# Causal attention with a squared-activation FFN on one core: narrow score jobs in plain f32, fixed right-aligned probability tiles, first values on ScalarE

## The chip, the core and the metric

The kernel runs on one core of a Trainium2 chip. The metric is the device time of one execution in microseconds. Before the change three runs took 1117.45, 1113.68 and 1116.32 us: the median is 1116.32 us. The profile was taken on a further execution of 1113.66 us, whose span from the first to the last instruction is 1111.9 us.

## The reference

```python
scores = scale * np.matmul(q, k.transpose(0, 1, 3, 2))         # B, H, S, D = 8, 8, 576, 64; f32
cum = np.cumsum(np.maximum(s, 0.0), axis=-1)
bias = -(cum[:, :, :, None] - cum[:, :, None, :])
scores = np.where(causal, -1000000000.0, scores + np.minimum(bias, 0.0))
attn = softmax(scores)                                         # max subtracted, sum + 1e-9
x = (attn @ v), heads side by side                             # 4608 tokens x 512
h = x @ w_in                                                   # 512 x 2048
g = np.where(h >= 1, h, np.where(h <= -1, 0.0, (h + 1) ** 2 / 4))
y = g @ w_out                                                  # 2048 x 512
```

## The kernel before

**FFN.** Operands are split into two f16 parts, high and low, and each product is three matmuls (high·high, high·low, low·high). The tokens of a batch are cut in two halves of 320 and 256 (`HALF`). For each half `ffn_h` makes 16 blocks of 12 matmuls into PSUM (line 531), ScalarE and VectorE make the activation from it (lines 543, 546, 547), ScalarE and GpSimd split it (lines 557, 558), and `ffn_y` uses it in 12 matmuls (line 570).

**Attention.** A job is a pair of heads and one half of the queries: 64 jobs, for each batch four *narrow* ones (half 0: query tiles of 64, 128 and 128 rows that see 64, 192 and 320 keys) and then four *wide* ones (half 1: two tiles that see 448 and 576 keys). A job has slots k = 0 to 7: preparation (`att_prep`, k = 0), values (`v_prep`, k = 1), six score units (`scores`, k = 2 to 7, one tile of one head, 576 keys in two pieces of 288); at k = 3 the loads of the next job are issued (`att_load`), at k = 7 the output of the previous job is made (`att_out`, "px", line 476).

**How scores are made precise.** Jobs 0 to 7 (batch 0) use plain f32: one matmul with 66 contraction rows, 64 of them q and k and two rows that add the cumulative bias (rows of 8 and -8 against cum; line 408). On the chip such a matmul appears as two weight loads and two matmul instructions. All later jobs use the reduced format f32r in two matmuls: Q1 and K1 of 128 rows (line 413) and Q2 and K2 of 68 rows (line 414). For that, q and k are loaded twice, into both halves of the partitions (line 338), ScalarE rounds them (lines 353, 356, 357), VectorE forms the remainders (lines 358, 361; in jobs 8 to 11 line 361 is on GpSimd), and two small DMAs on ScalarE's queue bring the bias rows from `cumd`. Q1, K1, Q2, K2 and the raw tiles rq, rk have one buffer each.

**After the score.** VectorE adds the mask, takes the minimum and writes a probability tile "p" (line 419), ScalarE takes the exponential (line 430). "p" rotates in four buffers, and GpSimd writes 64 zero columns behind each one's keys (line 403). `weights_t` scales and splits into "pb" (lines 451 to 457), a DMA transposes pb into "pt", and px multiplies pt by the transposed values "vt". Scores and px share two PSUM buffers "s".

**Start.** While the attention of batch 0 runs, the f64 weights are loaded in 16 + 16 chunks of 512 KB ("wir", "wor"), decoded and split (class `Weights`). `s` is loaded, cut at zero and summed along the row ("cum"); job 0 takes its bias rows straight from the SBUF tile, the later f32 jobs from the copy `cumf` in DRAM.

**Order.** Each engine runs its instructions in a fixed order that is made when the program is built: a list scheduler follows the program's order and the stated priorities (`high_priority`, `issue_after`). SyncE issues nearly all DMAs, in order, and an instruction of its queue that waits holds back those behind it.

## Time and profile before

| | |
|---|---|
| Median of three runs | 1116.32 us (1113.68 to 1117.45) |
| Profiled execution: time, span | 1113.66 us, 1111.9 us |
| Share of the span busy: PE, DVE, ACT, POOL | 91%, 77%, 66%, 61% |
| Mean granted TensorE clock | 0.961 |
| DMA moved | 155.12 MB |

The page lists for each engine its busy time in us. PE is TensorE's matmuls, PEld its weight loads, DVE VectorE, ACT ScalarE, POOL GpSimd, SP SyncE. In a timeline, a row gives the start in us from the span's start, the length in us, the engine, the line and operation, output<-input with its shape and the number of instructions that were merged (x). A bracket at the end is idle time of that engine just before the row and what ended it. Ends of matmuls are modelled: a matmul's bar is longer than the step to the next one, so bars overlap, and the step is what one costs.

### The profile page before, as it was taken

Reading aid. Unit: us, or ns where it says so; the run is one execution under the profiler, and the core shown is the slowest. Engines: PE = TensorE matmul, PEld = TensorE weight load, DVE = VectorE, ACT = ScalarE, POOL = GpSimd, SP = SyncE. Lnnn points to the kernel's source line nnn. Section 1 sums busy time; section 2 is a strip of 40 time slices with the busy share of each in tenths; the row PEclk is TensorE's granted clock in tenths of the full one; section 3 lists DMA queues with packets and bytes.
Section 4 is the critical chain, followed back from the end, with each engine's and each line's share of the span. In section 5 each row is a group of like instructions: output and inputs, shape, how many; then the busy total and the mean of one; then the engine's idle time right before and its main releaser. Section 6 shows DMA issues by size and latency. Waiting matters only on the chain.

```text
span 1111.9 us, 25079 instructions
## 1 busy us (share of the span) xinstructions
PE 1010.4 (91%) x8496; PEld 775.8 (70%) x8496; DVE 855.7 (77%) x2327; ACT 728.3 (66%) x1703; POOL 673.6 (61%) x1171
## 2 busy tenths in 40 slices
PE   3467798799999999999999999899999999899998
PEld 1234456587768877777778877787777877787787
DVE  7977896788777877877778877787778887887533
ACT  4556786677567774767567775877577765777432
POOL 4664677776557655676557755666467665766422
PEclk9956899699999999999999999999999999999999
DMA  7776753777558763878468763987377763776400
GB/s 228 176 195 172 189 142 91 158 165 156 106 111 184 158 146 74 182 147 175 89 126 185 149 148 73 184 165 155 80 161 163 168 137 77 159 155 137 68 25 20
DMA packets 340928, 155.12 MB, mean 140 GB/s; under 512 B 290984, under 2 KB 322572, under 8 KB 340800
## 3 DMA queue, kind: packets, MB, share of 16 engines
q1 hardware_dynamic: 331200, 143.68, 60.3%
q10 hardware_dynamic: 9600, 9.84, 2.8%
q8 instruction: 67, 1.10, 0.4%
q14 instruction: 61, 0.50, 0.2%
HBM read 72.28 MB, written 9.88 MB: 74 GB/s over the span
## 4 chain that ended last, share of the span: by engine, by line
PE 59%; DVE 15%; DMA 7%; issue 7%; ACT 6%; POOL 5%; SPq 0%; ACTq 0%; DVEq 0%; POOLq 0%
PE y L570 25%; PE h L531 24%; PE px L476 4%; PE s L413 3%; PE s L414 3%; DVE pb L457 3%; DMA pt<-pb 3%; DVE p L419 2%; DMA wir<-in_moe_w_in_dram 2%; DMA wor<-in_moe_w_out_dram 2%; ACT u L543 2%; DVE Q L358 2%; DVE h L546 2%; ACT p L430 2%; POOL pb L451 1%
## 5 line engine op out<-in xcount | busy, mean ns | idle before, releaser
L531 PE MATMUL h<-x,WI 128*128 128x256 f16 (+1 forms) x3072 | 465.2, 290 | 14.3 <-DVE u L547 7.1
L570 PE MATMUL y<-g,WO 128*128 128x256 f16 (+1 forms) x3072 | 455.6, 287 | 6.1 <-POOL g L558 4.8
L531 PEld LDWEIGHTS <-WI 128*128 128x128 f16 x3072 | 291.5, 99 | 106.4 <-issue 23.3
L570 PEld LDWEIGHTS <-WO 128*128 128x128 f16 x3072 | 287.5, 98 | 92.4 <-issue 14.4
L558 POOL TENSOR_TENSOR g<-u,g 128x320 f16<-128x320 f32 (+1 forms) x256 | 205.9, 804 | 149.3 <-ACT g L557 148.6
L430 ACT ACTIVATE p<-p,mn 64x64 f32<-64x64 f32 (+4 forms) x320 | 179.4, 561 | 144.0 <-DVE mn L419 131.2
L543 ACT ACTIVATE u<-h,ub,us 128x320 f32<-128x320 f32 (+1 forms) x256 | 149.2, 583 | 122.1 <-PE h L531 116.1
L451 POOL TENSOR_SCALAR pb<-p,rs 64x128 f16<-64x128 f32 (+4 forms) x160 | 97.5, 609 | 193.8 <-DVE rs L447 122.5
L546 DVE SCALAR_TENSOR_TENSOR h<-h,ws,u 128x320 f32<-128x320 f32 (+1 forms) x256 | 132.4, 517 | 102.3 <-ACT u L543 99.7
L454 POOL TENSOR_TENSOR pb<-p,pb 64x128 f16<-64x128 f32 (+4 forms) x160 | 170.3, 1064 | 9.4
L457 DVE SCALAR_TENSOR_TENSOR pb<-p,rs,pb 64x128 f16<-64x128 f32 (+4 forms) x160 | 138.4, 865 | 42.4 <-POOL pb L451 42.2
L419 DVE CUSTOM_DVE_ANT_0 p<-s,mask 64x64 f32<-64x64 f32 (+4 forms) x320 | 134.5, 421 | 27.4 <-PE s L414 23.7
L413 PE MATMUL s<-K,Q 128*64 128x64 f32 (+1 forms) x336 | 127.0, 379 | 15.7 <-DVE mn L419 8.7
L547 DVE SCALAR_TENSOR_TENSOR u<-u,r,h 128x320 f32<-128x320 f32 (+1 forms) x256 | 130.3, 509 | 6.8 <-DVE h L546 0.5
L452 ACT ACTIVATE p<-p,rs 64x64 f32<-64x64 f32 (+4 forms) x160 | 89.5, 560 | 56.7 <-DVE rs L447 55.8
L557 ACT CAST g<-u 128x320 f16<-128x320 f32 (+1 forms) x256 | 108.0, 422 | 6.3 <-DVE u L547 6.3
L414 PE MATMUL s<-K,Q 68*64 68x64 f32 (+1 forms) x336 | 103.8, 310 | 3.0 <-DMA K<-cumd 2.9
L453 POOL TENSOR_SCALAR pb<-p 64x128 f16<-64x128 f32 (+4 forms) x160 | 92.6, 579 | 14.4 <-ACT p L452 11.4
L476 PEld LDWEIGHTS <-vt 128*64 128x64 f16 x1536 | 73.7, 114 | 32.7 <-issue 27.9
L476 PE MATMUL px<-pt,vt 128*64 128x256 f16 (+3 forms) x1536 | 84.7, 260 | 10.6 <-DMA pt<-pb 9.1
L413 PEld LDWEIGHTS s<-K,Q 128*64 128x64 f32 (+1 forms) x336 | 62.1, 185 | 26.5 <-DVE mn L419 7.2
L414 PEld LDWEIGHTS s<-K,Q 68*64 68x64 f32 (+1 forms) x336 | 62.7, 187 | 6.2 <-ACT p L452 1.8
(107 smaller groups left out, 984.5 us busy)
## 6 DMA issues: line engine op xcount, KB each, us to landing
rk<-in_k_dram SPq DMA_DIRECT2D x56, 288.0 KB
v<-in_v_dram SPq DMA_DIRECT2D x32, 288.0 KB
rq<-in_q_dram SPq DMA_DIRECT2D x56, 160.0 KB
rk<-in_k_dram SPq DMA_DIRECT2D x56, 160.0 KB
wir<-in_moe_w_in_dram SPq DMA_DIRECT2D x16, 512.0 KB
wor<-in_moe_w_out_dram SPq DMA_DIRECT2D x16, 512.0 KB
rq<-in_q_dram SPq DMA_DIRECT2D x56, 128.0 KB
...
```

The costliest lines, as they stand in the source:

```text
L413: T.matmul(sc[:R, :c1 - c0], Q1[:, hd, qo:qo + R], K1[:, hd, c0:c1], start=True, stop=False)
L414: T.matmul(sc[:R, :c1 - c0], Q2[:KC, hd, qo:qo + R], K2[:KC, hd, c0:c1], start=False, stop=True)
L419: ttr[0] = V.tensor_tensor_reduce(out=Pt[:R, c0:c1], in0=sc[:R, :c1 - c0], in1=mask[:R, mo:mo + c1 - c0], scale=-0.125 if j < F32_JOBS els ...
L430: A.activation(Pt[:R, :W], Pt[:R, :W], AF.Exp, bias=m2[:R], scale=-1.0, accum_out=sums[n, i][:R, hd:hd + 1])
L454: G.tensor_tensor(los[1], pw, his[1], ALU.subtract)
L457: V.scalar_tensor_tensor(los[0], pv, rs[:R, :1], his[0], ALU.mult, ALU.subtract)
L476: T.matmul(px[hd * D:(hd + 1) * D, lo:N], VT[:, vl * NB + j, hd * D:(hd + 1) * D], PT[:, 4 * j + 2 * hd + pl, lo:], start=(m == 0), stop=( ...
L531: T.matmul(h[:, :N], WI[4 * kt + ft // 4][:, wl, ft % 4 * P:(ft % 4 + 1) * P], x[:, kt, xl], start=(n == 0), stop=(n == 3 * NKT - 1),)
L543: first = A.activation(u, h[:, :N], AF.Relu, bias=ubi[b], scale=usc[b][:, fg:fg + 1]).ins
L546: V.scalar_tensor_tensor(h[:, :N], h[:, :N], wsc[b][:, fg:fg + 1], u, ALU.mult, ALU.max)
L558: G.tensor_tensor(g[:, 1], u, g[:, 0], ALU.subtract)
L570: T.matmul(ys[b, hf, m][:, :N], WO[8 * (m // 2) + ft // 2][:, wl, c0:c0 + P], g[:, gl], start=(ft == 0 and n == 0), stop=(ft == NFT - 1 an ...
```

## The change

- **Narrow jobs of all batches in plain f32** (`in_f32`): jobs 0 to 7 as before, and now also the four narrow jobs of batches 1 to 7, 28 jobs. Each of their score units is one f32 matmul of 66 rows in place of the two f32r matmuls; they have no preparation and no second copy of q and k. Their two bias rows of q and of k come ready from a wider `cumf` (four rows for each head: cum, 8, -8, cum), in one DMA for q and one for k. Wide jobs of batches 1 to 7 stay as they were.
- **Loads in two buffers**: q and k of a job lie in one tile "qk" with two buffers, which takes the place of rq, rk and of the two fixed f32 pairs.
- **Probability tiles**: three fixed tiles PS (128, 512 and 640 columns, two heads each) in place of the rotating "p". Keys are right-aligned, so that the 64 zero columns always lie at the tile's end and are written once, at the start. Tiles of 64, 192, 320, 448 and 576 keys use PS 128, 512, 640, 512, 640.
- **First values**: in pairs 0 to 3 (batch 0) the scaled values are made by two ScalarE activations in place of two GpSimd operations.
- **Smaller ones**: `cx` holds the four rows of cum; Q1 and Q2 have 256 columns in place of 320; the last two weight tiles WO share their place with K1; `K_POOL` is gone (line 361 is always on VectorE).

```diff
-K_POOL = range(12)
...
-    QF, KF = [], []
-    for i, (tq, tk) in enumerate((("rq", "rk"), ("q1", "k1"))):
-        QF.append(ap.tile([P, 2, NQ], F32, tag=tq, bufs=1, name=f"QF{i}"))
-        KF.append(ap.tile([P, 2, S], F32, tag=tk, bufs=1, name=f"KF{i}"))
+    NQ1 = HALF[1][1]
+
+    def qk_tile(name, N, W):
+        t = ap.tile([P, 2 * (N + W)], F32, tag="qk", bufs=2, name=name)
+        q, k = t[:, :2 * N], t[:, 2 * N:]
+        return t, q.rearrange("p (h n) -> p h n", h=2), k.rearrange("p (h n) -> p h n", h=2)
+
+    first = qk_tile("qk_first", NQ, NQ)
...
+    cx = ap.tile([P, 4, S], F32, tag="pt", bufs=2, name="cx")
+    G.memset(cx[:BH, 1], 8.0)
+    G.memset(cx[:BH, 2], -8.0)
...
-    cumf = dp.tile([BH, S], F32, name="cumf")
+    cumf = dp.tile([BH, 4, S], F32, name="cumf")
...
-        nc.sync.dma_start(cumf, cum[:BH])
+        A.copy(cx[:BH, 3], cum[:BH])
+        nc.sync.dma_start(cumf, cx[:BH])
...
+    P_LEN = (P, 4 * P, 5 * P, 4 * P, 5 * P)
+    PS = {}
+    for w in sorted(set(P_LEN)):
+        PS[w] = cp.tile([P, 2, w], F32, name=f"PS{w}")
+        G.memset(PS[w][:, :, w - D:], 0.0)
...
+    def in_f32(j):
+        return j < F32_JOBS or jobs[j][1] == 0
...
+        t, q, k = qk_tile(f"qk{n}_{hf}", N, W) if j else first
+        raws[n, hf] = q, k
+        for t_, src, c0 in ((q, qT, q0), (k, kT, 0)):
+            sv = src[b, h0:h0 + 2, :, c0:W].rearrange("h d n -> d h n")
+            for d0 in (0,) if in_f32(j) else (0, D):
+                LOADQ.dma_start(t_[d0:d0 + D], sv)
+        if not in_f32(j):
             return
...
+            LOADQ.dma_start(q[D:KF32], cumf[2 * n:2 * n + 2, :2, q0:W].rearrange("h r n -> r h n"))
+            LOADQ.dma_start(k[D:KF32], cumf[2 * n:2 * n + 2, 2:, :W].rearrange("h r n -> r h n"))
...
-        if jobs.index((n, hf)) < F32_JOBS:
+        if in_f32(jobs.index((n, hf))):
             return
...
-        (G if jobs.index((n, hf)) in K_POOL else V).tensor_tensor(
-            K2[:D, :, :W], rk[:D], K1[:D, :, :W].bitcast(F32), ALU.subtract
-        )
+        V.tensor_tensor(K2[:D, :, :W], rk[:D], K1[:D, :, :W].bitcast(F32), ALU.subtract)
...
-        G.tensor_scalar(VB[:, 0, :S], v, r, 1.0, ALU.mult, ALU.mult)
-        if n < V_POOL:
-            G.tensor_scalar(v, v, r, 1.0, ALU.mult, ALU.mult)
+        if n >= V_POOL:
+            G.tensor_scalar(VB[:, 0, :S], v, r, 1.0, ALU.mult, ALU.mult)
+        else:
+            A.activation(VB[:, 0, :S], v, AF.Copy, scale=r)
+            A.activation(v, v, AF.Copy, scale=r)
             G.tensor_tensor(VB[:, 1, :S], v, VB[:, 0, :S], ALU.subtract)
...
-        if c0 == 0:
-            Pt = ap.tile([P, SP], F32, tag="p", bufs=4, name=f"p{n}_{i}_{hd}")
-            pbs[n, i].append(Pt)
-            G.memset(Pt[:R, W:W + D], 0.0)
-        Pt = pbs[n, i][hd]
+        Pt = PS[P_LEN[i]][:, hd, P_LEN[i] - D - W:]
...
-        if j < F32_JOBS:
-            T.matmul(
-                sc[:R, :c1 - c0], QF[j % 2][:KF32, hd, qo:qo + R], KF[j % 2][:KF32, hd, c0:c1], start=True, stop=True
-            )
+        if in_f32(j):
+            q, k = raws[n, i // 3]
+            T.matmul(sc[:R, :c1 - c0], q[:KF32, hd, qo:qo + R], k[:KF32, hd, c0:c1], start=True, stop=True)
         else:
```

What this does to the order is shown at three places. The first is VectorE in batch 4, from the end of the first narrow job (mn_2_1 is its last score unit) to the first units of the second (mn_0_0, mn_0_1). "ISA" rows are the mask-and-minimum operation of line 419 (now 424) and the read of its result; L358 and L361 are the remainders. Before:

```order
L419 ISA p_2_1_7881,mn_2_1_0_7886<-s_2_1_0_7883,mask 128x320
L419 ISA mn_2_1_0_7886 128x1
L358 SCALAR_TENSOR_TENSOR Q_1822<-rq_0_7772,Q_1822 64x640
L361 TENSOR_TENSOR K_107<-rk_0_7773,K_1823 64x2x320
L446 TENSOR_SCALAR rs_2_7890<-sm_2_7851 128x2
L447 RECIPROCAL rs_2_7890<-rs_2_7890 128x2
L419 ISA p_0_0_7985,mn_0_0_0_7990<-s_0_0_0_7987,mask 64x64
L419 ISA mn_0_0_0_7990 64x1
L457 SCALAR_TENSOR_TENSOR pb_2_7889<-p_2_0_7852,rs_2_7890,pb_2_7889 128x3x128
L488 SCALAR_TENSOR_TENSOR x_1_7154<-px_1_7897,ex_5561,x_1_7154 128x256
L419 ISA p_0_1_8014,mn_0_1_0_8019<-s_0_1_0_8016,mask 64x64
```

The same stretch after the change:

```order
L424 ISA mn_2_1_0_7602 128x1
L551 SCALAR_TENSOR_TENSOR h_1_0_7647<-h_1_0_7647,ws_6234,u_1_0_7661 128x256
L552 SCALAR_TENSOR_TENSOR u_1_0_7661<-u_1_0_7661,r_6224,h_1_0_7647 128x256
L451 TENSOR_SCALAR rs_2_7606<-sm_2_7573 128x2
L452 RECIPROCAL rs_2_7606<-rs_2_7606 128x2
L493 SCALAR_TENSOR_TENSOR x_0_7632<-px_0_7613,ex_7095,x_0_7632 128x320
L424 ISA PS_146,mn_0_0_0_7685<-s_0_0_0_7683,mask 64x64
L424 ISA mn_0_0_0_7685 64x1
L462 SCALAR_TENSOR_TENSOR pb_2_7605<-PS_150,rs_2_7606,pb_2_7605 128x3x128
L551 SCALAR_TENSOR_TENSOR h_1_1_7690<-h_1_1_7690,ws_6234,u_1_1_7703 128x256
L552 SCALAR_TENSOR_TENSOR u_1_1_7703<-u_1_1_7703,r_6224,h_1_1_7690 128x256
L424 ISA PS_146,mn_0_1_0_7711<-s_0_1_0_7709,mask 64x64
```

The remainders L358 and L361 are gone from between the two jobs; FFN work (L551, L552) and the other operations stand there in another order.

The second place is TensorE where batch 1 begins. Before, the last score units of batch 1's first narrow job stand one behind the other, directly ahead of the px of batch 0's last wide job (s is a score tile, px that output, pt its transposed weights):

```order
L413 MATMUL s_1_0_0_1907<-K_1823,Q_1822 128x192
L414 MATMUL s_1_0_0_1907<-K_107,Q_106 128x192
L413 MATMUL s_1_1_0_1932<-K_1823,Q_1822 128x192
L414 MATMUL s_1_1_0_1932<-K_107,Q_106 128x192
L413 MATMUL s_2_0_0_1961<-K_1823,Q_1822 128x320
L414 MATMUL s_2_0_0_1961<-K_107,Q_106 128x320
L413 MATMUL s_2_1_0_1971<-K_1823,Q_1822 128x320
L414 MATMUL s_2_1_0_1971<-K_107,Q_106 128x320
L476 LDWEIGHTS vt_666
```

After the change the units of that job, one matmul each, stand singly among the matmuls y of batch 0's FFN; here is one of them (s_1_0_0), and the px comes later:

```order
L575 LDWEIGHTS WO_136
L575 MATMUL y_0_3_1681<-g_0_8_1126,WO_136 128x320
L415 MATMUL s_1_0_0_1819<-qk_0_1603 128x192
L575 LDWEIGHTS WO_137
L575 MATMUL y_0_2_1680<-g_0_8_1126,WO_137 128x320
```

Between the last score of batch 0 (s_4_1_288 of its last job) and the px that uses it there were 20 FFN matmuls before, and there are 94 now.

The third place is the start of SyncE's queue (wir is a weight chunk, QF, KF or qk_first the tiles of job 0, cum or cx the row sums). Before:

```order
L120 DMA st<-in_s_dram 64x576
L322 DMA QF_77<-in_q_dram 64x2x320
L322 DMA KF_78<-in_k_dram 64x2x320
L190 DMA wir_155<-in_moe_w_in_dram 128x1024
L190 DMA wir_157<-in_moe_w_in_dram 128x1024
L190 DMA wir_159<-in_moe_w_in_dram 128x1024
L326 DMA QF_77<-cum 1x16x20
L327 DMA KF_78<-cum 1x16x20
L326 DMA QF_77<-cum 1x16x20
L327 DMA KF_78<-cum 1x16x20
L255 DMA v_0_161<-in_v_dram 128x576
```

After:

```order
L123 DMA st<-in_s_dram 64x576
L341 DMA qk_0_227<-in_q_dram 64x2x320
L341 DMA qk_0_227<-in_k_dram 64x2x320
L341 DMA qk_first<-in_q_dram 64x2x320
L341 DMA qk_first<-in_k_dram 64x2x320
L198 DMA wir_158<-in_moe_w_in_dram 128x1024
L347 DMA qk_first<-cx 1x16x20
L348 DMA qk_first<-cx 1x16x20
L347 DMA qk_first<-cx 1x16x20
L348 DMA qk_first<-cx 1x16x20
L198 DMA wir_160<-in_moe_w_in_dram 128x1024
L198 DMA wir_162<-in_moe_w_in_dram 128x1024
```

The load of s has moved to the front, and the second and third weight chunk stand behind the four bias rows, which wait for the row sums.

More of the change, by code (lines that the diff above doesn't have):

```diff
@@ L123, in attention_ffn @@
     V.memset(zr, 0.0)
-    V.memset(QF[0][D:KF32], 8.0)
-    V.memset(KF[0][D:KF32], -8.0)
+    V.memset(first[1][D:KF32], 8.0)
+    V.memset(first[2][D:KF32], -8.0)
+    cx = ap.tile([P, 4, S], F32, tag="pt", bufs=2, name="cx")
+    G.memset(cx[:BH, 1], 8.0)
+    G.memset(cx[:BH, 2], -8.0)
     V.tensor_scalar(st[:BH], st[:BH], 0.0, None, ALU.max)
-    cum = ap.tile([P, S], F32, tag="raw", name="cum")
+    cum = cx[:, 0]
     V.tensor_tensor_scan(cum[:BH], st[:BH], zr, 0.0, ALU.add, ALU.add)
-    cumf = dp.tile([BH, S], F32, name="cumf")
+    cumf = dp.tile([BH, 4, S], F32, name="cumf")
     cumd = dp.tile([BH, 2, S], F32, name="cumd")
@@ L148, in attention_ffn @@
     G.memset(ones, 1.0)
-    Q2 = cp.tile([P, 2, NQ], F32R, name="Q2")
+    Q1 = cp.tile([P, 2, NQ1], F32R, name="Q1")
+    Q2 = cp.tile([P, 2, NQ1], F32R, name="Q2")
     K2 = cp.tile([P, 2, S], F32R, name="K2")
@@ L163, in attention_ffn @@
     WI = [cp.tile([P, 2, NC], F16, name=f"WI{c}") for c in range(NW)]
-    WO = [cp.tile([P, 2, NC], F16, name=f"WO{c}") for c in range(NW + WO_LAG)]
+    WO = [cp.tile([P, 2, NC], F16, name=f"WO{c}") for c in range(NW)]
+    lag = ap.tile([P, WO_LAG, 2, NC], F16, tag="k1", bufs=1, name="WO_lag")
+    WO += [lag[:, i] for i in range(WO_LAG)]
     def flat32(t):
@@ L310, in attention_ffn @@
     NP = B * NPAIR
-    raws, pts_, vts, pbs, sums = {}, {}, {}, {}, {}
+    raws, pts_, vts, sums = {}, {}, {}, {}
+    def in_f32(j):
+        return j < F32_JOBS or jobs[j][1] == 0
     def att_load(n, hf):
@@ L318, in att_load @@
         j = jobs.index((n, hf))
[L319 to L339 removed]
+        t, q, k = qk_tile(f"qk{n}_{hf}", N, W) if j else first
[5 more added lines that the diff above has]
+        if not in_f32(j):
+            return
+        if j < CH_N:
+            for hd in range(2):
+                r = cum[2 * n + hd:2 * n + hd + 1]
+                LOADQ.dma_start(q[D:D + 1, hd], r[:, q0:W])
+                LOADQ.dma_start(k[D + 1:D + 2, hd], r[:, :W])
+        else:
+            LOADQ.dma_start(q[D:KF32], cumf[2 * n:2 * n + 2, :2, q0:W].rearrange("h r n -> r h n"))
+            LOADQ.dma_start(k[D:KF32], cumf[2 * n:2 * n + 2, 2:, :W].rearrange("h r n -> r h n"))
     def att_prep(n, hf):
[L343 removed]
+        if in_f32(jobs.index((n, hf))):
             return
         if not one:
[L346 removed]
             one.append(ap.tile([P, 2, S], F32R, tag="k1", bufs=1, name="K1"))
[L348 removed]
+        K1, = one
         rq, rk = raws.pop((n, hf))
@@ L420, in scores @@
                 out=Pt[:R, c0:c1], in0=sc[:R, :c1 - c0], in1=mask[:R, mo:mo + c1 - c0],
-                scale=-0.125 if j < F32_JOBS else -1.0, scalar=3.0e38 if mn is None else mn[:R],
+                scale=-0.125 if in_f32(j) else -1.0, scalar=3.0e38 if mn is None else mn[:R],
                 op0=ALU.add, op1=ALU.min, accum_out=m2[:R],
@@ L447, in weights_t @@
         V.reciprocal(rs[:R], rs[:R])
-        tiles2 = pbs.pop((n, i))
-        pv, pw = (Pt[:R, :W + D].rearrange("p (j c) -> p j c", c=P) for Pt in tiles2)
+        heads = [PS[P_LEN[i]][:R, hd, P_LEN[i] - D - W:] for hd in range(2)]
+        pv, pw = (t.rearrange("p (j c) -> p j c", c=P) for t in heads)
         his, los = ([PB[:R, :, 2 * hd + l, :] for hd in range(2)] for l in range(2))
         G.tensor_scalar(his[0], pv, rs[:R, :1], 1.0, ALU.mult, ALU.mult)
-        A.activation(tiles2[1][:R, :W], tiles2[1][:R, :W], AF.Copy, scale=rs[:R, 1:])
+        A.activation(heads[1][:, :W], heads[1][:, :W], AF.Copy, scale=rs[:R, 1:])
         G.tensor_scalar(his[1], pw, 1.0, 1.0, ALU.mult, ALU.mult)
```

28 lines of the change are left out of this document (2 added, 26 removed).

## The prediction

> **What bounds the kernel now.** I read the page's busy shares first, then the windows of three stretches (start, steady, last FFN): columns are the stretch, its length, and the busy us of PE, PEld, DVE, ACT and POOL.
>
> ```profile
> PE 1010.4 (91%) x8496; PEld 775.8 (70%) x8496; DVE 855.7 (77%) x2327; ACT 728.3 (66%) x1703; POOL 673.6 (61%) x1171
> 0.00:304.00 304.00, 231.23 (x1578) 156.81 (x1579) 244.58 (x622) 200.66 (x427) 193.78 (x310) 0.87 0.67 163
> 304.00:1041.00 737.00, 712.68 (x6339) 563.80 (x6337) 586.69 (x1658) 504.34 (x1224) 461.17 (x837) 1.00 0.67 141
> 1041.00:1112.00 71.00, 66.49 (x584) 55.23 (x582) 24.40 (x49) 23.30 (x53) 18.69 (x25) 0.99 0.10 27
> ```
>
> The steady stretch is six batches. PE is busy 712.7 of 737 us there at full granted clock (1.00), VectorE 80%, ScalarE 68%, GpSimd 63%: TensorE bounds it, and a microsecond of matmul that is added is paid in full unless it fills a wait. The first 304 us are different: VectorE leads (80%), PE is busy 76% at a clock of 0.87, and chains of latency count. In the last stretch there is no attention left, so the change does nothing there.
>
> So the question is which waits PE still has. The list of waits of PE in the steady stretch (us in total, times, longest):
>
> ```profile
> PE s L413 <- DVE Q L358: 6.3, 6, 1.7
> PE s L413 <- DVE mn L419: 6.0, 8, 1.2
> PE y L570 <- POOL g L558: 4.8, 6, 1.3
> PE s L414 <- DMA K<-cumd: 2.9, 2, 1.8
> PE px L476 <- DMA pt<-pb: 1.6, 2, 1.3
> PE px L476 <- DVE Q L358: 1.1, 1, 1.1
> ```
>
> They fill almost all of the 24.3 us in which PE is idle. Three of them (6.3, 2.9, 1.1) are the f32r preparation, and the 6.0 behind the minimum is its follower: VectorE runs in order, and in the first place shown above the remainders L358 and L361 stand ahead of the minimum that frees a score buffer. These two take
>
> ```profile
> L358 DVE SCALAR_TENSOR_TENSOR Q<-rq,Q 64x640 fp32r<-64x640 f32 x28 | 25.9, 925 | 2.5 <-ACT Q L353 1.6
> L361 DVE TENSOR_TENSOR K<-rk,K 64x640 fp32r<-64x640 f32 x24 | 19.9, 827 | 0.6
> ```
>
> **The price: f32 passes.** What a unit costs PE is the step from where the matmuls ahead of it end to the start of the next group. FFN steps first, then an f32r unit of 320 keys and one of 64, then an f32 unit of 448:
>
> ```profile
> 543.96 1.63 PE y L570 x12
> 605.94 1.47 PE L570 MATMUL y<-g,WO 128*128 128x256 f16 x12
> 607.25 0.27 PE L531 MATMUL h<-x,WI 128*128 128x256 f16 x1
> 569.79 0.84 PE L570 MATMUL y<-g,WO 128*128 128x320 f16 x5
> 570.36 0.42 PE L413 MATMUL s<-K,Q 128*128 128x320 f32 x1
> 570.62 0.30 PE L414 MATMUL s<-K,Q 68*128 68x320 f32 x1
> 570.77 1.12 PE L570 MATMUL y<-g,WO 128*128 128x320 f16 x7
> 564.36 0.71 PE L531 MATMUL h<-x,WI 128*128 128x320 f16 x4
> 564.79 0.30 PE L413 MATMUL s<-K,Q 128*64 128x64 f32 x1
> 564.93 0.22 PE L414 MATMUL s<-K,Q 68*64 68x64 f32 x1
> 564.99 1.27 PE L531 MATMUL h<-x,WI 128*128 128x320 f16 x8
> 110.74 0.92 PE L408 MATMUL s<-KF,QF 66*128 66x448 f32 x2
> 111.49 1.79 PE L531 MATMUL h<-x,WI 128*128 128x320 f16 x12
> L413 PEld LDWEIGHTS s<-K,Q 128*128 128x128 f32 x280 | 54.4, 194 | 14.6 <-PE s L414 4.5 <-DVE mn L419 3.7 <-DVE x L488 0.3
> ```
>
> An FFN matmul of 320 columns steps 1.63/12 = 0.136 us, one of 256 (607.25 - 605.94)/12 = 0.109. The five before the 320-key unit end at 569.79 + 5 x 0.136 = 570.47, so the f32r unit costs 570.77 - 570.47 = 0.30. The four before the 64-key unit end at 564.90: 0.09. By interpolation 192 keys cost 0.19. A narrow job (two heads) costs 2 x (0.09 + 0.19 + 0.30) = 1.16 us when nothing waits.
>
> The f32 unit of 448 keys steps 111.49 - 110.74 = 0.75 us, that is 1.67 ns a key: 0.11, 0.32 and 0.54 for the three narrow units, 1.93 us a job. This is the lower bound. The upper one lets each of a unit's two passes wait for a weight load of 0.194: 0.39, 0.39, 0.54, or 2.63 a job. At 448 keys no load shows at all, and the narrow units' weights are no bigger, so I stay near the lower end: 2.05. The increase is 0.89 us a job (0.77 to 1.47), for 28 jobs 24.9 us (21.6 to 41).
>
> Those short passes are where a rule weighs in. The Trainium skill, "TensorE: Matmul & The Clock Gate", section "The mechanism" (Part 3), says that a weight load overlaps running matmuls only if it goes to another row group. All passes here use the same rows; with every load of 0.194 in series a narrow f32 job would take 1.93 + 12 x 0.194 = 4.3 us, 2.2 more than the 2.05 I take, and the time would be 1101 + 28 x 2.2 = 1163. The row disagrees: two passes and two loads fit in 0.75 us, just the 448-column streaming. I give it 1 in 100.
>
> **The return: waits of the narrow jobs.** Lower bound, from the list: 6.3 + 6.0 + 2.9 + 1.1 = 16.3 us over 24 jobs, 0.68 a job. The list understates, since a matmul's bar is 0.30 long for a step of 0.136: each wait shows some 0.16 short. Upper bound, from a whole period:
>
> ```profile
> 912.42 1.63 PE y L570 x12
> 574.21 1.51 PE L476 MATMUL px<-pt,vt 128*64 128x256 f16 x30
> 575.65 0.24 PE L413 MATMUL s<-K,Q 128*64 128x64 f32 x1
> 611.69 0.94 PE L476 MATMUL px<-pt,vt 128*64 128x320 f16 x18
> 612.56 0.61 PE L531 MATMUL h<-x,WI 128*128 128x256 f16 x4
> ```
>
> The same piece of the chain comes at 543.96 and three batches later at 912.42: 122.8 us a batch. PE needs 384 x 0.136 + 384 x 0.109 = 94.1 for the FFN, 4 x (1.44 + 0.87) = 9.2 for px, 4 x 1.16 = 4.6 for the narrow scores, and scaled by columns (0.42 for 448, 0.27 for 288) 4 x 1.92 = 7.7 for the wide ones: 115.6. So 7.2 us a batch are lost, 1.8 a narrow job if all of it were theirs. Between 0.68 and 1.8 I take 1.2: the preparation waits and the hidden part of each, while waits for g and pt stay. Steady stretch: 24 x (0.89 - 1.2) = **-7.4 us**.
>
> **The start.** Batch 1 begins with PE idle:
>
> ```profile
> 194.57 0.63 PE L413 MATMUL s<-K,Q 128*128 128x320 f32 x1 [2.31 <-DVE mn L419]
> 202.15 2.77 PE L476 MATMUL px<-pt,vt 128*64 128x256 f16 x30 [5.62 <-DMA pt<-pb]
> 7.78 0.61 SPq L326 DMA_DIRECT2D QF<-cum  x1
> cumf<-cum SPq DMA_DIRECT2D x1, 144.0 KB
> ```
>
> In the second place shown, 94 FFN matmuls (12.8 us at 0.136) now lie between the last scores of batch 0 and their px, in place of 20 (2.7 us). They cover both waits: -7.9. The other three narrow jobs of batch 1 return less than a steady job each, -3 together; the four cost 4 x 0.89 = +3.6. In the first microseconds the third place counts: chunks two and three, issued before the bias row of 7.78, now go after four of them, a few us later; `cumf` grows from 144 to 576 KB, 432 KB more at the 163 GB/s of the start, 2.7 us of transfer. Against it the row sums start earlier, since s is loaded first. Bounds -1 and +6; I take +2. Sum of the start: -7.9 - 3 + 3.6 + 2 = **-5.3 us**.
>
> **Edits I cost at nothing.** Rows of the groups by shape:
>
> ```profile
> L403 POOL MEMSET p<- 128x64 f32 x256 | 34.6, 151 | 10.9 <-DVE pb L457 9.7
> L374 POOL TENSOR_SCALAR v<-v,rc 128x576 f32<-128x576 f32 x4 | 4.0, 992 | 0.2
> L452 ACT ACTIVATE p<-p,rs 128x576 f32<-128x576 f32 x32 | 24.8, 776 | 8.7 <-DVE rs L447 8.7
> ```
>
> The zero columns were 320 memsets of about 151 ns, 48 us of a GpSimd that is idle 39% of the span; FFN work hides them, and without that cover they would have been worth at most those few of them that PE feels. PS gives the narrow tiles three places in place of two and the wide ones two as before, so no new wait for a buffer. The values on ScalarE are 8 activations of about 0.78 us (nearest shape, L452), 6.2 us beside a ScalarE that is idle a third of the start; GpSimd loses operations of up to 0.99. Behind them on ScalarE wait exponentials and weight decodes: -1 to +2. Half the bytes of 28 loads go, at a DMA share of 0.67, and two buffers let them come a job earlier: 0, or up to the 1.6 us of waits for pt.
>
> **Sum.** 1113.66 - 7.4 - 5.3 = 1101.0. The profiled execution is 2.7 us below the median of 1116.32, about the spread of the runs, so I say 1102.
>
> **Rivals.**
> *The passes stay, the waits too (slower).* The waits behind the minimum may come from the two score buffers shared with px, not from the remainders; then only 6.3 + 2.9 + 1.1 = 10.3 us return, 0.43 a job. Steady: 24 x (0.89 - 0.43) = +11; with the start at 0, 1125; with loads in part exposed, 1139. It decides from a return under 0.89 a job. For it: 8 of the listed waits, 6.0 us, name the minimum and not the preparation. Against it: the order has VectorE free of the remainders just there. 20%.
> *The start takes it back.* Chunks come late to the engine that leads there (+6), y runs dry later in place of px (only -4 returned), the steady part is even: 1113.66 + 6 - 4 - 3 + 3.6 - 2 = 1114. 14%.
> *All lost time returns.* 24 x (0.77 - 1.8) = -25, start -9: 1080. Speaks for it: the units now stand singly between FFN groups. 10%.
> *Weight loads in series*, as above: 1163. 1%.
>
> **How the numbers follow.** My forecast (1088 to 1111) has 55%. Within 0.3% means 1113.0 to 1119.7, about what a measurement of this kernel can tell from no change. Faster is the forecast and the full return: 0.65. Same is the start's rival: 0.14. Slower is the first rival and the series of loads: 0.21. The range 1082 to 1127 leaves out about the lower half of the full return and the worse half of the slower cases.
>
> **What would show it.** Right: no wait of PE for Q or K in the list; 320-key f32 units stepping 0.54 us; a period under 122.8 us; PE idle at 190 to 215 us gone. Wrong: units of 64 and 192 keys stepping 0.39 (loads exposed); waits behind the minimum still 6 us or more; a first FFN matmul later than before; a period above 122.8.

## The result and the profile after

The changed kernel takes **1121.75 us** (median; 1119.29 to 1124.24, and 1129.54 in the profiled execution) against 1116.32 before. One more execution, of 1220.48 us at a mean granted clock of 0.857, belongs to a slower state and is left out of the range. The ratio is 1.0055, with a 95% interval of 1.0040 to 1.0070: slower, by about 6 us. The forecast was 1102. Measured again unmodified, beside the kernel before, it took 1126.88 against 1117.56, ratio 1.0079 (1.0054 to 1.0105).

The profiled execution lies 7.8 us above the median, so the second run's profile (1121.41) is read beside it. First the page of the changed kernel, busy time of each engine:

```profile
PE 1042.0 (92%) x8494; PEld 781.6 (69%) x8496; DVE 809.9 (72%) x2275; ACT 688.0 (61%) x1628; POOL 622.5 (55%) x842
```

VectorE, ScalarE and GpSimd each do 40 to 51 us less work than before; TensorE does 32 us more. Now the windows of the three stretches. So that the same work stands in each, the steady stretch is cut by the FFN itself: from 46.4 us after the first h matmul of batch 1 to 41.8 us after that of batch 7, which are the marks 304 and 1041 of before. The first three rows are the changed kernel, then the steady stretch of its second run:

```profile
0.00:298.60 298.60, 236.79 (x1580) 158.95 (x1582) 229.68 (x621) 198.90 (x424) 176.40 (x220) 0.89 0.71 163
298.60:1056.30 757.70, 739.22 (x6340) 568.07 (x6339) 556.74 (x1608) 466.02 (x1152) 429.84 (x600) 0.99 0.62 127
1056.30:1127.20 70.90, 66.05 (x578) 54.59 (x575) 23.45 (x47) 23.07 (x52) 16.24 (x23) 1.00 0.05 18
294.90:1048.10 753.20, 735.65 (x6340) 566.20 (x6339) 556.74 (x1608) 466.27 (x1152) 429.96 (x600) 1.00 0.62 128
```

The start is 5.4 us shorter (304.0 to 298.6; 9.1 in the second run). The steady stretch is 16.2 us longer in the second run: TensorE is busy 735.65 us in place of 712.68, **23.0 more**, and idle 17.5 in place of 24.3, only **6.8 less**. The forecast had 21.4 more and 28.8 less there: a return larger than all the idle time that the list showed.

What is left of the idle time is told by the list of waits of PE in the steady stretch of the changed kernel:

```profile
PE y L575 <- POOL g L563: 9.7, 6, 2.9
PE y L575 <- ACT g L562: 4.3, 7, 1.8
PE s L415 <- DVE mn L424: 2.3, 7, 0.5
PE px L481 <- DMA pt<-pb: 0.6, 1, 0.6
PE s L418 <- DVE mn L424: 0.5, 1, 0.5
```

Every wait for Q or K is gone, and the wait behind the minimum fell from 6.0 to 2.8. Scores and px waited 18.1 us before, now 3.4. But **y now waits 14.0 us for g** (13.7 in the second run), where it waited 6.0 before, 4.8 of them for GpSimd and the rest for ScalarE:

```profile
PE y L570 <- ACT g L557: 1.2, 6, 0.2
```

A new wait has come in place of the old ones, at other matmuls. It has two parts: for GpSimd's g 9.7 us (7.6 in the second run), for ScalarE's 4.3 (6.1).

**GpSimd's part.** Most of the 9.7 sits at one place, in five of the six batches: where the last narrow job gives way to the first wide one. The timeline of the changed kernel there (start, duration, engine; in brackets the wait ahead of it and for whom):

```profile
606.92 2.55 SPq L463 DMA_TRANSPOSE pt<-pb  x2
...
609.59 1.49 PE L536 MATMUL h<-x,WI 128*128 128x256 f16 x12
...
611.38 0.58 POOL L456 TENSOR_SCALAR pb<-PS,rs 128x384 f16<-128x384 f32 x1 [3.08 <-DMA pt<-pb]
...
612.53 1.09 POOL L459 TENSOR_TENSOR pb<-PS,pb 128x384 f16<-128x384 f32 x1
613.59 1.29 POOL L563 TENSOR_TENSOR g<-u,g 128x256 f16<-128x256 f32 x2
...
614.30 1.07 PE L575 MATMUL y<-g,WO 128*128 128x256 f16 x6 [2.15 <-POOL g L563]
615.66 2.57 PE L536 MATMUL h<-x,WI 128*128 128x256 f16 x11
```

There are two buffers pb for a narrow job's three query tiles, so the third tile (128x384) waits until the transpose of the first has read its buffer. In the trace GpSimd takes its work in order: behind that wait stand two splits of g, and y waits for the first. GpSimd waited for pt before as well, but y hardly behind it; the sums of the steady stretch are, before and in the second run:

```profile
POOL pb L451 <- DMA pt<-pb: 6.5, 6, 2.4
POOL pb L456 <- DMA pt<-pb: 8.2, 3, 3.1
```

In the first profile of the changed kernel it is 16.4. In the second run y waits for GpSimd at five turns, and GpSimd for pt ahead of three of them only.

**ScalarE's part.** It sits some 13 us earlier, where ScalarE rounds k for the first wide job. In the second run, last batch of the steady stretch:

```profile
961.24 0.70 PE L415 MATMUL s<-qk 66*128 66x320 f32 x2
961.97 0.62 SPq L341 DMA_DIRECT2D qk<-in_q_dram  x1
...
966.11 1.25 SPq L341 DMA_DIRECT2D qk<-in_k_dram  x2
...
971.17 1.15 ACT L367 CAST K<-qk 128x1152 fp32r<-128x1152 f32 x1 [1.95 <-DMA qk<-in_k_dram]
...
972.69 0.39 ACT L562 CAST g<-u 128x256 f16<-128x256 f32 x1
...
973.13 1.75 PE L575 MATMUL y<-g,WO 128*128 128x256 f16 x12 [1.64 <-ACT g L562]
```

An f32 score reads the load tile qk itself. So the load of the first wide job can go only after the last score of the narrow job that had its buffer (the bar ends at 961.94, the load goes at 961.97). By the trace it is such a score that releases this load in five of the six batches. ScalarE then waits for k, with the activation of the FFN behind it, and y waits for that. ScalarE's waits for k are 8.9 us in the steady stretch of the second run and were 0.2 before:

```profile
ACT K L367 <- DMA qk<-in_k_dram: 8.9, 6, 3.0
ACT K L356 <- DMA rk<-in_k_dram: 0.2, 1, 0.2
```

### The profile page after: what moved, and what is told of

It reads as the page before. It is cut to its first block, busy times and chain, and to the rows that moved or that the text cites. A ratio compares the mean times of both kernels' runs of the same rounds, so it can differ in the third digit from the quotient of the medians.

```text
span 1127.2 us, 24261 instructions
## 1 busy us (share of the span) xinstructions
PE 1042.0 (92%) x8494; PEld 781.6 (69%) x8496; DVE 809.9 (72%) x2275; ACT 688.0 (61%) x1628; POOL 622.5 (55%) x842
## 5 line engine op out<-in xcount | busy, mean ns | idle before, releaser
L435 ACT ACTIVATE PS<-PS,mn 64x64 f32<-64x64 f32 (+4 forms) x320 | 178.8, 559 | 143.6 <-DVE mn L424 115.4
L456 POOL TENSOR_SCALAR pb<-PS,rs 64x128 f16<-64x128 f32 (+4 forms) x160 | 106.7, 667 | 194.5 <-DVE rs L452 147.8
L551 DVE SCALAR_TENSOR_TENSOR h<-h,ws,u 128x320 f32<-128x320 f32 (+1 forms) x256 | 133.1, 520 | 108.3 <-ACT u L548 106.8
L462 DVE SCALAR_TENSOR_TENSOR pb<-PS,rs,pb 64x128 f16<-64x128 f32 (+4 forms) x160 | 132.2, 826 | 78.9 <-POOL pb L456 78.4
L459 POOL TENSOR_TENSOR pb<-PS,pb 64x128 f16<-64x128 f32 (+4 forms) x160 | 161.0, 1007 | 12.3
L424 DVE CUSTOM_DVE_ANT_0 PS<-s,mask 64x64 f32<-64x64 f32 (+4 forms) x320 | 134.1, 420 | 39.4 <-PE s L415 25.7
L552 DVE SCALAR_TENSOR_TENSOR u<-u,r,h 128x320 f32<-128x320 f32 (+1 forms) x256 | 130.3, 509 | 6.9
L415 PE MATMUL s<-qk 66*64 66x64 f32 (+4 forms) x420 | 123.6, 382 | 12.2 <-DVE mn L424 9.0
L457 ACT ACTIVATE PS<-PS,rs 64x64 f32<-64x64 f32 (+4 forms) x160 | 89.1, 558 | 53.8 <-DVE rs L452 52.9
L458 POOL TENSOR_SCALAR pb<-PS 64x128 f16<-64x128 f32 (+4 forms) x160 | 94.7, 592 | 17.9 <-ACT PS L457 15.0
L415 PEld LDWEIGHTS s<-qk 66*128 66x128 f32 (+1 forms) x420 | 63.7, 188 | 45.6 <-DVE mn L424 19.4
L418 PE MATMUL s<-K,Q 128*128 128x448 f32 (+1 forms) x168 | 69.8, 416 | 0.5 <-DVE mn L424 0.5
```

What stands on the lines that cost most here:

```text
L415: T.matmul(sc[:R, :c1 - c0], q[:KF32, hd, qo:qo + R], k[:KF32, hd, c0:c1], start=True, stop=True)
L424: ttr[0] = V.tensor_tensor_reduce(out=Pt[:R, c0:c1], in0=sc[:R, :c1 - c0], in1=mask[:R, mo:mo + c1 - c0], scale=-0.125 if in_f32(j) else - ...
L435: A.activation(Pt[:R, :W], Pt[:R, :W], AF.Exp, bias=m2[:R], scale=-1.0, accum_out=sums[n, i][:R, hd:hd + 1])
L459: G.tensor_tensor(los[1], pw, his[1], ALU.subtract)
L462: V.scalar_tensor_tensor(los[0], pv, rs[:R, :1], his[0], ALU.mult, ALU.subtract)
L551: V.scalar_tensor_tensor(h[:, :N], h[:, :N], wsc[b][:, fg:fg + 1], u, ALU.mult, ALU.max)
```

## The experiments

Every run is compared with the kernel before on the same chip; ratios have a 95% interval. Four theories are told apart. **A**: the new wait of y comes from loads that now stand ahead of the transposes in SyncE's queue, since two buffers let them go earlier. **B**: the f32 passes cost more than the preparation returns. **C**: the fixed probability tiles cost something. **D**, formed later: the return is real, but y's wait for the split of g takes its place.

**Again, and with one part undone each.** The first kernel is the unmodified changed kernel.

> The changed kernel again, for a second profile: the one at hand was taken on an execution of 1129.5 us, 7.8 us above the median. Theory A (queue): where a batch turns from narrow to wide jobs, SyncE has the loads of two wide jobs and a value tile (about 1.25 MB) ahead of the transposes of the last narrow job; these land late, GpSimd waits for its pb buffer with the FFN's split behind it, and TensorE waits 1 to 3 us for it once a batch. A expects that wait of y for g at all six places again, 1 us or more each. Theory B (passes): the f32 units of 64 keys cost 0.26 us and more, and the narrow jobs cost TensorE 0.3 to 0.4 us more each than in f32r with all its waits; B expects the same cost of the units, and that the wait at the turn is small in a typical run. Both expect a ratio of 1.004 to 1.007 and 1119 to 1124 us.

The second puts the narrow jobs back into f32r and keeps all else:

```diff
-    Q1 = cp.tile([P, 2, NQ1], F32R, name="Q1")
-    Q2 = cp.tile([P, 2, NQ1], F32R, name="Q2")
+    Q1 = cp.tile([P, 2, NQ], F32R, name="Q1")
+    Q2 = cp.tile([P, 2, NQ], F32R, name="Q2")
...
-        return j < F32_JOBS or jobs[j][1] == 0
+        return j < F32_JOBS
```

> The changed kernel with the narrow jobs of batches 1 to 7 in f32r again (two matmuls, preparation, double loads); two buffers, fixed tiles and first values stay. B expects it faster than the changed kernel by 24 x 0.36 = 9 us or more: 1112 or less. A expects the loads to run ahead as before and the waits of the preparation to come back, so no gain: 1118 to 1128, with y still waiting for g at the turn to the wide jobs.

The third holds all loads of batches 1 to 7 behind the transposes (`tps` keeps the last one):

```diff
-            nc.sync.dma_start_transpose(
+            tps[0] = nc.sync.dma_start_transpose(
...
+                with tc.issue_after(tps[0]) if j >= F32_JOBS else ExitStack():
-                att_load(*jobs[j + 1])
+                    att_load(*jobs[j + 1])
```

> The changed kernel with the loads of q and k queued on SyncE behind the last transpose that the program has issued by then (from job 8 on). A expects the wait of y for g at the turn gone (under 0.5 us) and with it its half clock, 1.5 to 2.6 us a batch over six batches: 1106 to 1113 us. B expects no change, 1119 to 1124. If the loads then come late, waits of TensorE for qk appear and it is slower.

The fourth brings back the rotating probability tiles with their 320 memsets:

```diff
-        Pt = PS[P_LEN[i]][:, hd, P_LEN[i] - D - W:]
+        if c0 == 0:
...
+            Pt = ap.tile([P, SP], F32, tag="p", bufs=4, name=f"p{n}_{i}_{hd}")
...
+            G.memset(Pt[:R, W:W + D], 0.0)
```

> The changed kernel with the rotating probability tiles again, zero columns written by GpSimd for each (320 memsets of about 0.15 us, 48 us of GpSimd). A and B: within 2 us of the changed kernel, 1119 to 1125. Theory C (the fixed tiles cost the time, through waits for the three places): 1112 to 1117.

Measured: unmodified 1.0079 (1.0054 to 1.0105); f32r 1119.81, 1.0028 (1.0010 to 1.0046); loads held 1150.41, 1.0303 (1.0280 to 1.0327); rotating tiles 1124.89, 1.0068 (1.0047 to 1.0090). The fixed tiles are worth nothing either way, as forecast, so C falls. In the unmodified kernel the wait of y for GpSimd came again at the turn, 0.9 to 2.3 us in five of six batches. f32r wins back some 6 us by the ratios, where B expected 9 or more, so B holds in part. With f32r y waits 1.0 us for ScalarE and 10.8 for GpSimd, and ScalarE not at all for k: ScalarE's part of the new wait goes with the f32 jobs, GpSimd's does not. Holding the loads cured nothing: they then come too late (ScalarE waits 33.1 us for k), and the scores wait for K, which ScalarE copies from the load:

```profile
PE s L419 <- ACT K L367: 10.4, 10, 1.7
PE y L577 <- POOL g L565: 9.2, 12, 3.7
```

**The wait at the turn taken away.** Each narrow query tile gets a buffer pb of its own, in the same memory; then the kernel before with the same edit.

```diff
-        PB = ap.tile([P, i + 1, 4, P], F16, tag=f"pb{hf}", ...)
+        PB = ap.tile([P, i + 1, 4, P], F16, tag="pbw" if hf else f"pb{i}", bufs=2 if hf else 1, ...)
```

> The changed kernel, but each of the three narrow query tiles of a job has a weight-split tile pb of its own (1, 2 and 3 KB a partition) in place of two shared ones of 3 KB: the same SBUF, and GpSimd no longer waits at the third one for the transpose of the first, which at the narrow-to-wide turn stands behind seven loads. No load and no transpose is moved. Theory A (the turn carries the loss: GpSimd waits there for pt, the FFN split is queued behind it, and y waits for the split): GpSimd's waits of pb for pt (8.2 to 16.4 us in the steady stretch) fall under 2, TensorE's waits of y for GpSimd's g (7.6 to 9.7) under 4, and the time falls by 6 batches x 1.2 to 2 us = 7 to 12 us, to 1112 to 1117 where the unmodified changed kernel took 1124 to 1127. Theory B (the f32 passes cost more than the preparation returned, and that alone is the loss): the waits move but the time falls by 3 us at most.

> The kernel before with the same three tiles pb of their own. GpSimd's waits of pb for pt are 6.5 us in its steady stretch and y's for GpSimd's g 4.8. Theory A (the wait was brought by the change): little to win here, -4 to +1 us, 1113 to 1119. Theory B says the same; the run is the baseline for the one before it: if it wins as much as that, the wait is not of the change.

(In these two expectations A stands for the wait at the turn, whatever brings it.) Measured: 1112.35, ratio 0.9967 (0.9947 to 0.9987), 10 to 13 us under the unmodified changed kernel by the ratios; but the kernel before wins as much: 1106.42, 0.9908 (0.9885 to 0.9931), against the expectation. By that expectation the wait would not be of the change. The windows part the two. In the changed kernel 9.6 us come out of the steady stretch, and PE's list has no wait for GpSimd's g left; ScalarE's part stays. Its steady row, and the first of the list:

```profile
296.50:1040.10 743.60, 735.03 (x6343) 566.31 (x6342) 551.05 (x1609) 466.36 (x1152) 429.15 (x600) 1.00 0.63 130
...
PE y L575 <- ACT g L562: 6.2, 5, 2.0
```

In the kernel before the steady stretch wins only 1.8 us (737.0 to 735.2), and 4.7 us come out of the start (the first h matmul of batch 1 at 252.9, not 257.6). So what came with the change is that y waits behind GpSimd's wait for pb in the steady stretch; the edit is good for both kernels, at different places.

**The price of the short unit, and the values.** The 64-key f32 matmul is issued twice; and the values of pairs 0 to 3 go back to GpSimd.

```diff
-            T.matmul(sc[:R, :c1 - c0], q[:KF32, ...], k[:KF32, ...], start=True, stop=True)
+            for _ in range(2 if i == 0 else 1):
+                T.matmul(sc[:R, :c1 - c0], q[:KF32, ...], k[:KF32, ...], start=True, stop=True)
```

> The changed kernel with the f32 score matmul of the 64-key unit issued twice into the same buffer (64 more of them: 32 narrow jobs x 2 heads), with the same result. Theory B by the price on record (0.11 us, streaming alone): +7 us, 1132. Theory B by the step seen in the changed kernel's trace (0.26 at least, a fixed cost of a short f32 matmul): +17 us, 1142. Theory A says nothing on the price; if the passes lie in waits of TensorE that are there anyway, +3 or less.

> The changed kernel with the values of pairs 0 to 3 back on GpSimd, as before. The start of the changed kernel is 5.5 to 9 us faster by the mark of the first FFN matmul of batch 1 (257.6 us before, 248.5 to 252.2 after). If the values on ScalarE carry that: the mark goes back by 4 us or more, and the time to 1129 to 1133. If the earlier row sums and the single write of the sums carry it: the mark and the time stay within 2 us, 1123 to 1128.

Measured: doubled 1133.43, ratio 1.0154 (1.0126 to 1.0182). That is 0.9% above the unmodified kernel (1.0055 to 1.0079), some 10 us for 64 matmuls or 0.15 us each, nearer to the forecast's 0.11 than to the 0.26 and more that a single one steps. In the steady stretch PE's busy time grows by 5.1 us for 48 of them, 0.11 each. The rows agree: single in the second run of the changed kernel, with its weight loads, then doubled (four passes) here.

```profile
560.95 0.57 PE L575 MATMUL y<-g,WO 128*128 128x320 f16 x3
561.45 0.19 PEld L415 LDWEIGHTS s<-qk 66*64 66x64 f32 x2 [0.26 <-issue]
561.45 0.33 PE L415 MATMUL s<-qk 66*64 66x64 f32 x2
561.71 0.99 PE L575 MATMUL y<-g,WO 128*128 128x320 f16 x6
```

```profile
575.80 0.45 PE L416 MATMUL s<-qk 66*64 66x64 f32 x4
576.18 1.05 PE L537 MATMUL h<-x,WI 128*128 128x256 f16 x8
```

A single unit steps 561.71 - 561.45 = 0.26 us from its own start, two of them 0.38: the repeat adds 0.12. Counted as the forecast counts, the single unit costs more: the three y matmuls ahead of it end at 560.95 + 3 x 0.136 = 561.36, its weight load starts only at 561.45, and so it takes 561.71 - 561.36 = 0.35 us. Some 0.24 of that is not paid again by a repeat of the same matmul; what a unit with other operands would pay there isn't tested. The values back on GpSimd: 1128.29, 1.0102 (1.0078 to 1.0127), and batch 1's first h matmul at 254.8, between the two expectations. The unmodified kernel had 252.2 and 248.5. So the values on ScalarE seem to carry 3 to 5 us of the gain at the start, though the intervals overlap and the two profiles of the same kernel differ by as much.

**f32 alone, the second buffer alone, the return alone.** First the f32r kernel with tiles pb of its own. Then the changed kernel with one load buffer for the wide jobs (`at` alternates for f32 jobs and is 0 for the others; loads keep the order of jobs):

```diff
-        t = ap.tile([P, 2 * (N + W)], F32, tag="qk", bufs=2, name=name)
+        t = ap.tile([P, 2 * (N + W)], F32, tag=f"qk{at}", bufs=1, name=name)
...
+        t, q, k = qk_tile(f"qk{n}_{hf}", N, W, j % 2 if in_f32(j) else 0) if j else first
...
+                with tc.issue_after(ldq[0]) if j > F32_JOBS else ExitStack():
```

Then the kernel before without the narrow preparation, with shared tiles pb and with its own:

```diff
+            for d0 in (0, D) if hf or j == F32_JOBS else (0,):
...
+        if hf == 0 and jobs.index((n, hf)) > F32_JOBS:
+            A.activation(Q1[:D, :, :1], rq[:D, :, :1], AF.Copy, scale=0.125)
+            A.copy(K1[:D, :, :1], rk[:D, :, :1])
+            return
```

> The changed kernel with three tiles pb of its own (as the run that took 1112.35) and with the narrow jobs of batches 1 to 7 back in f32r with their preparation; loads in two buffers, fixed probability tiles and the start stay as changed. Against that run it tells the f32 passes alone. Theory B (the passes cost more than the preparation returned): 4 to 7 us faster, 1105 to 1108, steady period 123 to 124 us (124.5 there, 123.0 in the kernel before with tiles of its own). If the passes pay for themselves once the turn is free: the same or slower, 1112 to 1118.

> The changed kernel, shared tiles pb kept, but the wide jobs of batches 1 to 7 use only one of the two load buffers (the narrow ones alternate, loads in the order of jobs). The third wide job's load then stands behind the last narrow transpose and the first wide one in SyncE's queue, not ahead of them. Theory A (the loads ahead make the transposes late): GpSimd's waits of pb for pt (8.2 to 16.4 us) fall under 5, y's waits for GpSimd's g (7.6 to 9.7) under 5, the time falls by 5 to 10 us to 1115 to 1120. Rival (it is the single buffer that comes late now, as when all loads were held behind the transposes): ScalarE's waits for the loads of k grow from 8.9 us to 15 or more and the time stays at 1123 to 1130. Rival (place in the queue does not matter): all three stay.

> The kernel before, f32r passes kept, without the preparation of 27 narrow jobs (batches 1 to 7, all but the first): their high parts, remainders L358 and L361, bias loads and the doubled half of the loads are left out, only one column of the high parts is copied so that the order of loads stays. Their scores are computed from the operands of an earlier job. It shows the return alone, with no price. By the forecast's term (1.2 us a job): -32 us, 1085. By the waits in the list alone (0.43 to 0.68): -11 to -18, 1099 to 1107. By the difference of the two runs with tiles pb of their own (a price of 0.96 a job by streaming, 1.5 us a batch of loss left, so a return of about 0.6): -16, 1101.

> The kernel before without the preparation of 27 narrow jobs, as the run that took 1110.86, and with three tiles pb of its own. In that run TensorE's loss around the scores and px fell by 4.8 us a batch, but its loss between two FFN matmuls rose by 2.1. Theory C (the return is real, and a wait of y for GpSimd's split takes its place, since GpSimd holds the split behind pb): with the tiles of its own the FFN loss falls back to 1.4 a batch or less, and the time to 1085 to 1095, 11 to 21 below the kernel before with tiles of its own (1106.42). Rival (the return is small in itself): the tiles win their 11 us here too but no more, or less: 1098 to 1102, 4 to 8 below it.

(What that last expectation calls theory C is D here.) Measured, with what PE did in the steady stretch (us; waits from its list), beside the f32r kernel of above:

```
kernel                        median   ratio  (95%)             steady  busy   idle  y and h  s and px
before                        1116.32                           737.0   712.7  24.3    6.0     18.1
changed, second run           1126.88  1.0079 (1.0054-1.0105)   753.2   735.7  17.5   14.1      2.8
changed, f32r                 1119.81  1.0028 (1.0010-1.0046)   749.9   718.0  31.9   12.1     19.5
changed, own pb               1112.35  0.9967 (0.9947-0.9987)   743.6   735.0   8.6    6.2      1.8
changed, own pb, f32r         1100.54  0.9860 (0.9842-0.9878)   736.0   712.4  23.6    6.0     17.1
changed, one wide buffer      1125.71  1.0078 (1.0056-1.0099)   754.2   738.8  15.4   14.2      0.6
before, own pb                1106.42  0.9908 (0.9885-0.9931)   735.2   713.6  21.6    8.4     12.9
before, no preparation        1110.86  0.9938 (0.9917-0.9958)   731.3   712.6  18.7    9.5      8.5
before, no prep., own pb      1101.54  0.9870 (0.9847-0.9893)   727.2   713.0  14.2    6.4      7.2
```

The rows with "own pb" and "own pb, f32r" differ in the narrow jobs alone, f32 passes against f32r with its preparation: busy 22.6 us more, scores and px 15.3 less. **The f32 jobs cost 22.6 and return 15.3.** The waits of y sum to the same, though 6.2 of them are for ScalarE with f32 and 4.9 for GpSimd with f32r. The stretch is 7.6 us longer with f32 and the start 3.8 (first h matmul of batch 1 at 250.1 against 246.3), of 11.8 us on the whole time. With shared tiles pb it is otherwise: there the edits other than f32 make the stretch 12.9 us longer (737.0 to 749.9, in that trace some of it at a lower clock, 0.99), and f32 adds 3.3. One buffer for the wide jobs puts the third load behind the transposes, and nothing changes: GpSimd still waits 12.1 us for pt, ScalarE 9.5 for k, and y 13.9, 8.5 of them for ScalarE; the time stays at 1125.71, where A expected 1115 to 1120. So the loads ahead in the queue are not the cause, and **A falls**. Without any preparation, at no price, the kernel before wins 7 us with shared tiles (the scores and px return 9.6, y takes 3.5 back) and 5 with its own: far from the 32 of the forecast. With shared tiles that is less than any expectation; with its own it is what the rival expected (the return is small in itself, 1098 to 1102), not D (1085 to 1095). In the last row y takes nothing back (6.4 after 8.4), and still only 5.7 us return at scores and px. So the first half of D, a large return that y's wait hides, falls; what is left of it is y's new wait.

**y given more time.** Open was whether y waits for the split alone, or the engines behind it are late on the whole. y is put three FFN steps behind h:

```diff
-Y_LAG = 2
+Y_LAG = 3
```

> The changed kernel, with y three FFN steps behind h in place of two (Y_LAG 3), so that ScalarE and GpSimd have one group of 12 matmuls (1.3 to 1.6 us) more to finish g. By the split of TensorE's loss per batch (f32 streaming +3.84, loss at scores and px -2.8, loss between FFN matmuls +1.9): if the third term is y's wait for the split, y's waits for g (13.7 us in the steady stretch) fall under 4, the loss between FFN matmuls from 2.8 to about 1 a batch, and the time by 8 to 13 us to 1112 to 1117. Rival (the engines behind are late on the whole, and a longer lag only moves the wait): the waits show up at h, px or scores instead, and the time stays at 1121 to 1127.

> The kernel before with the same lag of three. Its loss between FFN matmuls is 0.9 us a batch and its waits of y for g 6.0 us in the steady stretch. If y's wait is what the change added, there is less to win here: 0 to -5 us, 1112 to 1118. If it wins as much as the changed kernel, the wait is not of the change.

> The fastest version so far (the changed kernel with f32r narrow jobs and tiles pb of their own, 1100.54) with a lag of three. Loss between FFN matmuls 1.9 us a batch, waits of y for g 4.9: -3 to -8 us, 1092 to 1098, if the lag frees them; 1099 to 1102 if they only move.

> The changed kernel with both remedies: tiles pb of their own (1112.35 alone) and the lag of three (1111.31 alone), each about 13 us below the unmodified changed kernel. If both remove the same wait (GpSimd holds the split of g behind its wait for pt, and y waits for the split), they do not add: 1108 to 1113. If they remove two different losses, they add to 1098 to 1103.

Measured: changed 1111.31, ratio 0.9956 (0.9941 to 0.9971); before 1118.81, 1.0024 (1.0008 to 1.0040); f32r with tiles of its own 1101.12, 0.9864 (0.9841 to 0.9888); changed with both remedies 1112.06, 0.9959 (0.9942 to 0.9977). With a lag of three the changed kernel is the faster one of the two. Its list of PE's waits, steady stretch:

```profile
PE s L415 <- DVE mn L424: 6.8, 10, 1.3
PE s L418 <- DVE mn L424: 1.3, 2, 1.0
PE px L481 <- DMA pt<-pb: 1.0, 1, 1.0
PE px L481 <- DVE h L551: 0.5, 1, 0.5
PE s L415 <- DVE x L493: 0.5, 1, 0.5
PE y L575 <- POOL g L563: 0.5, 2, 0.2
```

y's wait is gone (0.5 us), a part of it has moved to the minimum (8.1 us, from 2.8 and 2.2 in the two profiles without the lag), and the stretch is 743.5 us long, 9.7 less than in the second run. In the kernel before the lag also cuts the waits of y and h (6.0 to 2.0), but those of scores and px rise from 18.1 to 19.7, and the time is a little longer, not 0 to 5 us shorter. So what the lag wins, it wins on the wait that came with the change: **D holds** for that part. f32r with tiles of its own wins nothing by it, as expected where waits only move. And the two remedies do not add (1112.35, 1111.31, together 1112.06), though they do not remove the same: the tiles take GpSimd's part of y's wait and leave ScalarE's (6.2 us), the lag takes both. With both, y waits 0.7 us and the scores 12.4 behind the minimum, in an execution 4.9 us above its median; so it seems to have moved there.

## Why the prediction was wrong, point by point

- **What bounds the kernel**: right. TensorE's busy time and waits account for the steady stretch: +23.0 busy, -15.3 at scores and px, +8.1 at y and h make +15.8 of the 16.2 us seen between the kernel before and the second run.
- **The price of the f32 passes**: inside its bounds (0.77 to 1.47), but too low. 0.89 a job was forecast; PE's busy time grew by 23.0 us over 24 jobs, 0.96. Units of 320 and 192 keys step 0.54 and 0.33 as said:

```profile
551.73 0.49 PE L415 MATMUL s<-qk 66*128 66x192 f32 x2
552.06 0.71 PE L575 MATMUL y<-g,WO 128*128 128x320 f16 x4
552.61 0.70 PE L415 MATMUL s<-qk 66*128 66x320 f32 x2
553.15 0.84 PE L575 MATMUL y<-g,WO 128*128 128x320 f16 x5
```

  The one of 64 costs 0.35 where 0.11 was taken, near the 0.39 of exposed loads. By these steps a job is 2 x (0.35 + 0.33 + 0.54) = 2.44 us, between the 2.05 taken and the upper bound of 2.63, and the price 2.44 - 1.16 = 1.28. Why the busy time, with its modelled ends, gives less isn't told apart. By the Trainium skill, "TensorE: Matmul & The Clock Gate", section "The mechanism" (Part 3), a weight load overlaps running matmuls only if it goes to another row group; with all loads in series the estimate was 4.3. The trace disagrees.
- **The return of the waits: the step that failed.** "Between 0.68 and 1.8 I take 1.2: the preparation waits and the hidden part of each, while waits for g and pt stay." Neither half held. The waits at scores and px returned 15.3 us over 24 jobs, 0.64 each, what the list had shown (0.68). If the price is counted by steps, the return must be too: 24 x 1.28 + 8.1 - 16.2 = 22.6 us, an estimate of 0.94 a job. By either count it is under 1.2 and about a third of a microsecond under its price, where the forecast had it 0.31 above. So of the 7.2 us a batch that were missing in the period, 2.6 to 3.8 were the narrow jobs', not 4.8. And the waits for g did not stay: 6.0 became 14. Of the increase 3.1 to 4.9 us are for ScalarE behind the late load of k and 2.8 to 4.9 for GpSimd (second run and first profile differ). After these 8.1 us only 0.30 a job came back by the list (7.2 us), not 1.2.
- **Edits at nothing**: for the fixed tiles right (rotating tiles 1124.89, the unmodified kernel 1121.75 and 1126.88). Half loads and two buffers have no run of their own. But all edits other than f32 together were not nothing: with f32r narrow jobs and shared tiles pb the steady stretch is 12.9 us longer than before, and y waits 10.8 us for GpSimd in place of 4.8. With tiles pb of their own in both kernels it is 0.8 us (736.0 against 735.2). The values on ScalarE were taken as -1 to +2 and seem to bring 3 to 5.
- **The start**: -5.3 was forecast, -5.4 and -9.1 were measured; that the sum comes near is luck. In its parts: the px of batch 0's last job no longer waits (5.62 before), and the scores of batch 1's first job wait 0.59 in place of 2.31; but that job's own px waits 2.00. That is 5.3 us of the 7.9 expected. The two waits that are left there:

```profile
196.53 0.81 PE L415 MATMUL s<-qk 66*128 66x320 f32 x2 [0.59 <-DVE mn L424]
199.33 1.65 PE L481 MATMUL px<-pt,vt 128*64 128x320 f16 x18 [2.00 <-DVE rs L452]
```

  The first microseconds were taken as 2 us later; the first h matmul came at 41.9, not 51.2. What takes the rest up again isn't told apart. The start is also 7.5 us shorter with f32r narrow jobs (mark at 250.1), so it does not hang on the f32 passes.
- **The rivals**: the one at 1125 came nearest in time, by another mechanism: it had the waits behind the minimum stay, and they fell to less than half. Its condition came true in this form: the return stayed under the price that was measured. No rival had a new wait of y in the steady stretch.
- **What would show it**: no wait for Q or K, 0.54 for 320 keys, the idle time at 190 to 215 us cut though not gone, minimum under 6: nearly all as said. The period named as the test of the sum, 122.8, went the wrong way: the steady stretch of six batches is 753.2 us in the second run, 125.5 a batch.

**What stays open**: which edit makes y wait for GpSimd at the turn. GpSimd's wait for pt is 6.5 us before, 17.7 with f32r, 8.9 with rotating tiles, 12.1 with one wide buffer, 4.9 without preparation. None of these edits alone brings y's wait or takes it away. And why less returns at scores and px in the kernel before without preparation (9.6 and 5.7 us) than by the f32 passes (15.3) isn't told apart.

The experiments point to a version that beats both kernels: the change without its f32 passes, with tiles pb of their own, 1100.54 us (ratio 0.986). Its steady stretch is 736.0 us, hardly shorter than before; by the profiles its gain lies in the start, where batch 1's first h matmul comes at 246.3, 11.3 us earlier.

## What to carry to other kernels

Where one engine is busy 97% of a stretch, weigh added work on it against the waits that the list shows at the places concerned, and count price and return in the same way: what the period seems to lose beyond the list need not belong to the part that is removed. When a wait goes, look for the next engine whose queue holds both a blocked operation and one that the bound engine needs (here GpSimd, the third pb ahead of the split of g, and ScalarE, the rounding of a late k ahead of its g), and price that too. When matmuls read a load tile directly, ask how much longer they hold its buffer, and whose load comes late by it. A cheap slack there can decide the sign of the change, so try both kernels with it before the change is dropped: with one more step of lag the changed kernel was the faster one here (1111.31 against 1118.81), while one more buffer helped both alike.
